# Attention with an MLP behind it: keys in three tiles of 128, and the last 64 keys of a whole batch as block-diagonal tiles

## The chip, the cores and the metric

The kernel runs on one core of a Trainium2 chip. The metric is the device time of one execution in microseconds (us); lower is better. The core has five engines with a queue each: TensorE (PE; its weight loads are listed as PEld), VectorE (DVE), ScalarE (ACT), GpSimd (POOL) and SyncE (SP), which here only issues DMAs. TensorE writes to PSUM, eight banks of 512 float32 a partition; everything else lies in SBUF.

## The reference

There are 8 batches of 12 heads with 448 tokens of 64 features. Queries and keys are normalized by their root mean square and scaled by g_q and g_k; softmax attention follows; the heads of a token are put together to 768 features; and an MLP with a gated activation ends it.

```python
def rmsnorm(x, g):
    rms = np.sqrt(np.mean(x * x, axis=-1, keepdims=True) + 1e-06)
    return x / rms * g
q_n, k_n = (rmsnorm(q, g_q), rmsnorm(k, g_k))
scores = scale * np.matmul(q_n, k_n.transpose(0, 1, 3, 2))
attn = np.exp(scores - max) ; attn = attn / sum          # over the keys
x = np.matmul(attn, v)                                   # then (8 * 448, 12 * 64)
h = x @ w_in                                             # 768 -> 2048
g = h * np.clip(h + 3.0, 0.0, 6.0) / 6.0
out = g @ w_out                                          # 2048 -> 768
```

## The kernel before

**Pairs of heads.** The unit of the attention is a pair of heads, six pairs to a batch (NJ = 6), 48 in all (P = 0 to 47). The two heads share the 128 partitions after the transposition, 64 features each.

**Stages of a pair.** `loads` (L295) brings K and Q into one tile qk and V into vf, token p*4 + t on partition p, so 112 partitions (PT) with four tokens each (T). `prep` (L310) squares K and Q (L320 to L330), sums the squares over the 64 features (L337), makes the inverse root on ScalarE (L343, L344), scales into bfloat16 qks (L351) and casts V into va (L359), which has a column of ones behind the 64 features, so that AV gives the sum of the exponentials too. `turn` (L365) turns qks so that features lie on partitions: for the first ten pairs (NPE) by TensorE (L377), for the others by a DMA transpose from SP (L388); the keys are then multiplied by g_q g_k into kp (L381 or L392). `attend` (L402) makes the scores transposed, keys on partitions: four tiles of 112 keys by 448 queries, the two heads as two matmuls in 64 rows of the array each (L416), and takes the exponential of both heads at once (L421, 112 partitions by 896). From batch 1 on two tiles are put in one step ("size = 2"), which takes both buffers of S. `gather` (L429) multiplies the exponentials by V (L437): for each of four slices of 128 queries, four key tiles for two heads, eight matmuls with 65 columns. The first three slices go to X; the last, of which only the upper 64 queries are new, goes to R, which is shared by three pairs. VectorE divides by the sums (L462, L463 for X of each pair; L502, L503 for R of three pairs), and the result is turned to xT (by TensorE in batch 0, by DMA transposes after, L486, L511). The 64 last tokens of two batches share one 128-token tile of the MLP, so even batches have 384 columns of h, odd ones 512.

**MLP.** `h_group` (L525): 16 groups a batch of six matmuls (L533), with the activation on ScalarE (L539) and VectorE (L541). `y_group` (L550): six or eight groups a batch of 16 matmuls (L558), copied by VectorE (L566) and stored by SP (L585). While batch b is in attention, TensorE's time is filled with h of batch b-1 and y of batches b-2 and b-1; what is left after the last attention runs alone at the end.

**Order.** Every piece of work is a step with a duration, a due time and the steps it depends on (class `Plan`). `order` (L68) simulates the engines with these durations and gives each engine's instructions in the order that comes out; the engines then run strictly in that order, each waiting by semaphores for what it needs. The due times come from `begin[P]`: START, then FIRST for each pair of batch 0, and after it the MLP time of the batch over six plus PAIR. `Ring` hands out buffers in turn, and the step that takes one waits for all users of what was in it. The weights of the MLP are loaded by GpSimd in eight parts (L277, L283), from W_IN_AT and W_OUT_AT on. `spare` (L599) gives the PSUM banks of the attention to the MLP at its end.

PSUM before: S two buffers of two banks, X and R one buffer of one bank each, M two of one bank.

Of the kernel before, what the change touches and what calls it, by code (L numbers as in the profile page):

```python
# [33 lines left out]
class Plan:  # L34
# [33 lines left out]
    def order(self):  # L68
# [8 lines left out]
        soft = []  # L77
# [13 lines left out]
        while len(done) < len(self.steps):  # L91
# [14 lines left out]
            for x in s.on:  # L106
                open_[x].remove(s)
            s.eng, s.start = e, at
# [3 lines left out]
            if s.xfer:  # L112
# [5 lines left out]
                else:  # L118
                    dma_free = self.hard(soft, max(dma_free, s.end), s.xfer)
                    s.end = dma_free + self.DMA_LATENCY + s.late  # L120
            done.append(s)
# [23 lines left out]
def kernel(  # L145
# [24 lines left out]
    NP = B * NJ  # L170
    assert PT == 112 and S - SM == 64 and D == 64 and NKT == NJ and B % 2 == 0
# [8 lines left out]
    mark = const.tile([1, 1], FP32, name="mark")  # L180
    ident = const.tile([128, 128], BF16, name="ident")
# [3 lines left out]
    qk_r = Ring(tiles("qk", 5, [128, 2, 2, T * D], FP32))  # L185
    vf_r = Ring(tiles("vf", 5, [128, 2, T * D], FP32))
    sq_r = Ring(tiles("sq", 2, [128, 2, 2, T * D], FP32))
    ssq_r = Ring(tiles("ssq", 4, [128, 4 * T], FP32))
    rs_r = Ring(tiles("rs", 4, [128, 4 * T], FP32))
    qks_r = Ring(tiles("qks", 3, [128, 2, T, 2, D]))  # L190
    kq_r = Ring(tiles("kq", 4, [128, 2, S]))
    kp_r = Ring(tiles("kp", 3, [128, S + 16]))
    va_r = Ring(tiles("va", 5, [128, 2, T, E1]))
    e_r = Ring(tiles("e", 3, [128, T, 2, S]))
    xn_r = Ring(tiles("xn", 3, [128, NS, 2, D]))
    rd_r = Ring(tiles("rd", 3, [128, NS, 2], FP32))
# [6 lines left out]
    X_r = Ring(tiles("X", 1, [128, 512], FP32, psum))  # L203
    R_r = Ring(tiles("R", 1, [128, 512], FP32, psum))
# [6 lines left out]
    GATE, W_IN_AT, W_OUT_AT, W_STEP = 2, 7.0, 35.0, 6.3  # L211
    START, FIRST, PAIR = 9.0, 4.1, 2.3
    LEAD = 4
    HURRY = 0.8
# [27 lines left out]
    for P in range(NP):  # L242
        b = P // NJ
        begin.append(begin[-1] + (FIRST if b == 0 else (
            sum(x[3] for x in seq[b]) / NJ + PAIR + (1.1 if (P + 2) < NPE else 0.0))))
    begin += [begin[-1] + 8.0 * (i + 1) for i in range(8)]

# [15 lines left out]
    def make_ones():  # L263
        for t in va_r.bufs:
            nc.gpsimd.memset(t[:, :, :, D:E1], 1.0)
        for t in kp_r.bufs:
            nc.gpsimd.memset(t[:, S:S + 16], 0.0)

    g_load = add("ACT", 2.2, 0, load_g, after=1.5, late=3.0)
    g_make = add("DVE", 0.1, 0, lambda: nc.vector.scalar_tensor_tensor(  # L270
        out=gp[:], in0=gq_t[:], scalar=8.0, in1=gk_t[:], op0=MULT, op1=MULT), g_load, after=7.5)
    id_make = add("POOL", 0.5, 0, make_ident)
    one_make = add("POOL", 0.6, 0, make_ones)
# [17 lines left out]
    def heads(src, P):  # L291
        b, j = divmod(P, NJ)
        return src[b, 2 * j:2 * j + 2, :, :].rearrange("h (p t) d -> p h (t d)", t=T)

    def loads(P):  # L295
        at = begin[P]
        qk, war, use = qk_r.take()
        res = []
        cost = 0.62 if P < 3 else 0.85
        for i, src in enumerate((k, q)):  # L300
            e = "ACT" if i and P < 3 else "SP"
            res.append(add(e, 0.47, at - 26, lambda i=i, src=src, e=e: {"ACT": nc.scalar, "SP": nc.sync}[e].dma_start(
                out=qk[0:PT, i], in_=heads(src, P)), *war, xfer=cost, after=max(0.7, at - 24)))
        L[P] = (qk, use, res)
        vf, war, use = vf_r.take()
        s = add("SP", 0.47, at - 19, lambda: nc.sync.dma_start(
            out=vf[0:PT], in_=heads(v, P)), *war, xfer=cost, after=max(0.7, at - 20))
        V[P] = (vf, use, s)

    def prep(P):  # L310
        at = begin[P]
        hurry = HURRY if P < NJ else 1.0
        qk, qk_use, ld = L.pop(P)
# [3 lines left out]
        def square(e, i):  # L317
            o, x = sq[0:PT, i], qk[0:PT, i]
# [5 lines left out]
        halves = P < 2 * NJ  # L324
# [72 lines left out]

    AV, XT, R = {}, {}, {}  # L400

    def attend(P):  # L402
        b, j = divmod(P, NJ)
# [270 lines left out]
```

## Time and profile before

| what | us |
|---|---|
| median of 7 runs (440.61 to 443.31) | 441.18 |
| the profiled execution | 442.12 |
| its span, first to last instruction | 440.2 |
| TensorE busy, matmuls | 412.3 (94%) |
| VectorE busy | 245.2 (56%) |
| ScalarE busy | 248.8 (57%) |
| GpSimd busy | 240.6 (55%) |
| exponentials L421, 192 of 914 ns | 166.2 |
| scaling L351 on GpSimd, 87 of 1060 ns | 90.9 |
| squares L329 on GpSimd, 36 of 1892 ns | 68.1 |
| sums L337 on VectorE, 47 of 1214 ns | 57.1 |

Busy time counts how long an engine had at least one instruction in it. For TensorE matmuls overlap in the pipeline and their ends are modelled; so what a matmul costs is read from the distance between starts. A line of the timeline gives start, duration, engine (SPq and ACTq are the queues that issue DMAs), source line, operation, output<-input with sizes, the count, and in brackets how long the engine idled before it and on what. In the chain of waits each line is a start, a duration and what was the last to end there. The granted clock of TensorE was 0.996 of full.

### The profile page before, as it was taken

To read this page: it belongs to the slowest core of one execution; us is meant where nothing else is said; L and a number is where in the kernel's file an instruction comes from. 1 tells how busy PE (TensorE), PEld (TensorE's weight loads), DVE (VectorE), ACT (ScalarE), POOL (GpSimd) and SP (SyncE) were. 2 spreads that over 40 slices of the span, in tenths; PEclk is the share of its full clock that TensorE was granted. 3 is DMA by queue.
4 is the path that set the end of the run, shared out by engine and by line. 5 is a ranking of instruction groups with operands and counts; after the bars stand their busy time and mean duration, and the time that the engine had idled before them with its cause. 6 is when DMAs were issued, how large, how long until landed. Compare 5 with 4: busy or idle time off the path is not lost.

```text
span 440.2 us, 9224 instructions
## 1 busy us (share of the span) xinstructions
PE 412.3 (94%) x3682; PEld 229.1 (52%) x3682; DVE 245.2 (56%) x417; ACT 248.8 (57%) x425; POOL 240.6 (55%) x230
## 2 busy tenths in 40 slices
PE   0687889999999999999999999999999999999996
PEld 0355445555455565554455555554455555654563
DVE  1998777657664564456565465456564444334421
ACT  3788578557775676357673677457673665123200
POOL 3499899765857657665766666746757510000000
PEclk9999899999999999999999999999999999999999
DMA  8999999988464746674456655684466320220122
GB/s 233 251 264 259 228 222 195 191 191 206 104 141 131 187 118 141 150 213 126 116 163 166 163 140 156 159 209 117 107 162 175 95 57 11 56 80 0 37 71 73
DMA packets 102923, 64.58 MB, mean 147 GB/s; under 512 B 59744, under 2 KB 99424, under 8 KB 102880
## 3 DMA queue, kind: packets, MB, share of 16 engines
q1 hardware_dynamic: 94544, 57.01, 51.6%
q0 software_dynamic: 7296, 6.29, 8.9%
q10 hardware_dynamic: 1040, 0.69, 0.5%
q8 instruction: 29, 0.48, 0.5%
q14 instruction: 14, 0.11, 0.1%
HBM read 45.61 MB, written 11.01 MB: 129 GB/s over the span
## 4 chain that ended last, share of the span: by engine, by line
PE 76%; DVE 7%; POOL 5%; issue 5%; ACT 3%; DMA 3%; SPq 1%; POOLq 0%; DVEq 0%
PE M L558 25%; PE M L533 24%; PE S L416 8%; PE X L437 7%; PE S L558 4%; PE S L533 2%; DVE ssq L337 2%; POOL sq L329 2%; PE R L437 2%; ACT e L421 2%; DMA qk<-in_k_dram 1%; DVE qks L351 1%; POOL qks L351 1%; PE X L558 1%; DVE sq L322 1%
## 5 line engine op out<-in xcount | busy, mean ns | idle before, releaser
L421 ACT ACTIVATE e<-S 112x896 bf16<-112x896 f32 x192 | 166.2, 914 | 64.9 <-PE S L416 64.9
L533 PE MATMUL M<-xT,w_in_sb 128*128 128x384 bf16 (+1 forms) x696 | 147.9, 351 | 3.8 <-DVE gT L541 3.8
L351 POOL TENSOR_TENSOR qks<-qk,rs 112x512 bf16<-112x512 f32 x87 | 90.9, 1060 | 89.0 <-ACT rs L344 88.9
L558 PE MATMUL M<-w_out_sb,gT 128*128 128x384 bf16 x736 | 131.8, 326 | 0.0
L558 PEld LDWEIGHTS <-gT 128*128 128x128 bf16 x896 | 82.9, 98 | 57.8 <-issue 7.8
L533 PEld LDWEIGHTS <-w_in_sb 128*128 128x128 bf16 x768 | 69.8, 98 | 69.2 <-issue 14.5
L541 DVE SCALAR_TENSOR_TENSOR gT<-t,M 128x384 bf16<-128x384 f32 (+1 forms) x116 | 70.7, 611 | 59.9 <-ACT t L539 59.1
L539 ACT ACTIVATE t<-M 128x384 f32<-128x384 f32 (+1 forms) x116 | 62.6, 540 | 68.7 <-PE M L533 65.2
L437 PEld LDWEIGHTS <-e 112*128 112x128 bf16 x1536 | 64.9, 99 | 31.4 <-issue 16.0
L337 DVE TENSOR_REDUCE ssq<-sq 112x16 f32<-112x1024 f32 (+1 forms) x49 | 58.3, 1192 | 24.4 <-POOL sq L329 12.0
L329 POOL TENSOR_TENSOR sq<-qk 112x1024 f32<-112x1024 f32 x36 | 68.1, 1892 | 0.0
L416 PE MATMUL S<-kq,kp 64*128 64x448 bf16 x384 | 56.6, 364 | 3.9 <-DVE kp L381 1.7
L437 PE MATMUL X<-va,e 112*128 112x65 bf16 x1152 | 58.4, 195 | 0.8 <-ACT e L421 0.6
L566 DVE COPY y<-M 128x384 f32<-128x384 f32 x46 | 25.6, 556 | 59.3 <-PE M L558 59.1
L359 POOL CAST va<-vf 112x512 bf16<-112x512 f32 x48 | 31.6, 659 | 9.0 <-DMA vf<-in_v_dram 7.2
L392 POOL TENSOR_SCALAR kp<-kq,gp 128x448 bf16<-128x448 bf16 x23 | 32.3, 1402 | 5.6 <-DMA kq<-qks 5.6
L463 DVE TENSOR_TENSOR xn<-X,rd 128x384 bf16<-128x384 f32 x48 | 26.7, 557 | 1.6
L416 PEld LDWEIGHTS <-kp 64*128 64x128 bf16 x384 | 12.3, 94 | 28.0 <-issue 19.0
L437 PE MATMUL R<-va,e 112*128 112x65 bf16 x384 | 20.4, 195 | 0.0
L377 PE MATMUL M<-ident,qks 112*128 112x112 bf16 x80 | 7.8, 238 | 13.0 <-DVE qks L351 12.4
L558 PE MATMUL S<-w_out_sb,gT 128*128 128x384 bf16 x112 | 19.5, 326 | 0.0
L462 DVE RECIPROCAL rd<-X 128x6 f32<-128x6 f32 x48 | 9.2, 191 | 15.8 <-PE X L437 15.8
(42 smaller groups left out, 155.0 us busy)
## 6 DMA issues: line engine op xcount, KB each, us to landing
qk<-in_k_dram SPq DMA_DIRECT2D x48, 224.0 KB, 3.4
vf<-in_v_dram SPq DMA_DIRECT2D x48, 224.0 KB, 3.6
qk<-in_q_dram SPq DMA_DIRECT2D x45, 224.0 KB, 3.6
w_in_sb<-in_moe_w_in_dram POOLq DMA_DIRECT2D x4, 768.0 KB, 11.7
w_out_sb<-in_moe_w_out_dram POOLq DMA_DIRECT2D x4, 768.0 KB, 10.8
out_dram<-y SPq DMA_DIRECT2D x8, 336.0 KB, 3.1
out_dram<-y SPq DMA_DIRECT2D x8, 288.0 KB, 3.2
out_dram<-y SPq DMA_DIRECT2D x8, 240.0 KB, 3.6
```

The source lines that it names most:

```text
L329: parts = [add("POOL", 1.93, at - 10, lambda: nc.gpsimd.tensor_tensor(out=sq[0:PT], in0=qk[0:PT], in1=qk[0:PT], op=MULT), *ld, *war, lock= ...
L337: red = add("DVE", 0.6 * n, at - 8 * hurry + 0.5 * i0, lambda i0=i0, i1=i1, cs=cs: nc.vector.tensor_reduce(out=ssq[0:PT, cs], in_=sq[0:PT, ...
L351: sc.append(add(on, 0, at - 6 * hurry, lambda e, i=i, rs4=rs4: engines[e].tensor_tensor(out=qks[0:PT, i].rearrange("p t h d -> p h t d"), ...
L359: vc = add({"POOL": 0.61}, 0, at - 3, lambda e: engines[e].tensor_copy(out=va[0:PT, :, :, 0:D], in_=vf[0:PT].rearrange("p h (t d) -> p h t ...
L392: nc.vector if e == "DVE" else nc.gpsimd).tensor_scalar_mul(
L416: nc.tensor.matmul(out=ps[:, a, 0:S], lhsT=kp[rows, c0:c0 + 128], rhs=kq[rows, 1, :], start=True, stop=True)
L421: x = add("ACT", 0.93, at + step * (t0 + i) / T + 0.2, lambda t=t0 + i, ps=ps: nc.scalar.activation(out=e[0:PT, t], in_=ps[0:PT, :, 0:S], ...
L437: nc.tensor.matmul(out=dst[:, a * E1:(a + 1) * E1], lhsT=e[0:PT, t, a, c0:c0 + 128], rhs=va[0:PT, a, t, :], start=(first and a == 0 and t ...
L533: nc.tensor.matmul(out=m[:, 0:n], lhsT=w_in_sb[:, kt, f * 128:(f + 1) * 128], rhs=X[:, kt, :], start=(kt == 0), stop=(kt == NKT - 1))
L539: r = add("ACT", 0.08 + n / 1200, due + span, lambda: nc.scalar.activation(out=t[:, 0:n], in_=m[:, 0:n], func=RELU, bias=0.5, scale=1.0 / ...
L541: g = add("DVE", 0.12 + n / 960, due + span, lambda: nc.vector.scalar_tensor_tensor(out=G[:, f, :], in0=t[:, 0:n], scalar=1.0, in1=m[:, 0: ...
L558: nc.tensor.matmul(out=m[:, 0:HALF], lhsT=G[:, f, i * 128:(i + 1) * 128], rhs=w_out_sb[:, f, cols], start=(f == 0), stop=(f == NFT - 1))
```

## The change

K and V are no longer dealt out as four tiles of 112 keys. The first 384 keys of a head form three tiles of 128 (token p*3 + t on partition p); the last 64 keys of all twelve heads of a batch are loaded, normalized and turned together, once a batch. For these, each pair gets a tile `kb` of 128 features by 128 keys that is zero outside two blocks, head 0 in the upper left and head 1 in the lower right, so that one matmul with all 128 rows gives the scores of both heads' rest keys, head 0 on partitions 0 to 63, head 1 on 64 to 127. Their AV runs as 64-row matmuls, one head in each half of the array, in the same step as a cluster of scores, and opens the accumulation in X. X now has two banks (one for each head) with all four slices, and R is gone. Q stays in four tiles of 112 queries.

From batch 1 on, two pairs are planned together: a cluster of two score tiles, one of the rest keys of both pairs (both in one S tile, one exponential), and two more of two tiles. The normalization of the last slice comes with each pair. In the planner, DMAs of SP and ACT wait for the eighth before them; the loads of the g vectors come first on ACT; Q of pair 0 is loaded from SP; odd pairs are prepared earlier by 0.7 of a pair's time; START stays at 9.0, FIRST goes from 4.1 to 3.7, PAIR from 2.3 to 2.1, W_IN_AT from 7 to 6, W_OUT_AT from 35 to 33.

```diff
+            if s.xfer and e != "POOL":
+                at = max(at, lanes[-8])
...
+                    lanes.append(s.end)
...
-    X_r = Ring(tiles("X", 1, [128, 512], FP32, psum))
-    R_r = Ring(tiles("R", 1, [128, 512], FP32, psum))
+    X_r = Ring(tiles("X", 1, [128, 2, 512], FP32, psum))
...
-    g_load = add("ACT", 2.2, 0, load_g, after=1.5, late=3.0)
+    g_load = add("ACT", 1.95, -99, load_g, after=0.7, late=1.0)
...
-            e = "ACT" if i and P < 3 else "SP"
+        e = "ACT" if 0 < P < 3 else "SP"
...
+    def rest_loads(b):
...
+            x = src[b, :, SM:S, :].rearrange("(j h) p d -> h p j d", h=2)
+            return [add("SP", 0.5, at, lambda a=a: nc.sync.dma_start(out=dst[a * 64:a * 64 + 64], in_=x[a]), *war,
+                        xfer=0.7, after=max(0.7, begin[b * NJ] - 30)) for a in range(2)]
...
+    def rest_prep(b):
...
+            q1 = add("POOL", 0.8, at - 12, lambda: nc.gpsimd.tensor_tensor(
+                out=sqr[:], in0=kr[:], in1=kr[:], op=MULT), *kl, *war, lock=True)
+        red = add("DVE", 0.47, at - 8 * hurry + 3, lambda: nc.vector.tensor_reduce(
+            out=rsr[:, 0:NJ], in_=sqr[:], axis=AX_X, op=ADD), q1, *rwar)
...
+        mk = add("DVE", 0.1, at - 6 * hurry + 3, lambda: nc.vector.tensor_tensor(
+            out=rm, in0=rsr[:, NJ:2 * NJ].unsqueeze(2).to_broadcast([128, NJ, 2]),
+            in1=head[:].unsqueeze(1).to_broadcast([128, NJ, 2]), op=MULT), r, head_make, lock=True)
+        on = {"DVE": 0.9} if b == 0 else {"DVE": 0.9, "POOL": 1.6}
+        sc = add(on, 0, at - 6 * hurry + 3, lambda e: (nc.vector if e == "DVE" else nc.gpsimd).tensor_tensor(
+            out=krs[:], in0=kr[:].unsqueeze(2).to_broadcast([128, NJ, 2, D]),
+            in1=rm.unsqueeze(3).to_broadcast([128, NJ, 2, D]), op=MULT), mk, *kwar, lock=True)
...
+            tr = add("SP", 1.3, at - 6, lambda: nc.sync.dma_start_transpose(
+                out=kb[:], in_=krs[:].rearrange("p j h d -> p (j h d)")), sc, *bwar, xfer=1.4, late=1.5)
+            ks = add("DVE", 0.47, at - 2, lambda: nc.vector.tensor_scalar_mul(
+                kb[:].rearrange("p j c -> p (j c)"), kb[:].rearrange("p j c -> p (j c)"), gp[:, 0:1]), tr, g_make,
+                lock=True)
...
+    def rest_keys(P):
...
+            for s in range(NS + 1):
+                c0 = s * 128 if s < NS else S - 128
+                for a in range(2):
+                    rows = slice(a * 64, a * 64 + 64)
+                    nc.tensor.matmul(
+                        out=X[:, a, s * E1:(s + 1) * E1], lhsT=er[rows, i, c0:c0 + 128], rhs=var[rows, P % NJ, :],
+                        start=(s == 0), stop=False, skip_group_check=True)
...
+    def attend_two(P, part):
+        step = (begin[P + 2] - begin[P]) / 7
+        if part == 0:
+            open_pair(P)
+            attend([[[(P, 0)], [(P, 1)]]], (0, P - 1), begin[P], step)
+        else:
+            open_pair(P + 1, (AV[P][2], AVR[P], AV[P][3]))
+            for cluster, extra, x in (
+                    ([[(P, NS), (P + 1, NS)]], None, POS[0]),
+                    ([[(P, 2)], [(P + 1, 0)]], (0, P), POS[1]),
+                    ([[(P + 1, 1)], [(P + 1, 2)]], None, POS[2])):
+                attend([cluster], extra, begin[P] + x * 7 * step, step)
...
-        size = 1 if P < NJ else 2
-        for t0 in range(0, T, size):
...
             for a in range(2):
-                for t in range(T):
+                for t in range(NS):
                     nc.tensor.matmul(
-                        out=dst[:, a * E1:(a + 1) * E1], lhsT=e[0:PT, t, a, c0:c0 + 128], rhs=va[0:PT, a, t, :],
-                        start=(first and a == 0 and t == 0), stop=(t == T - 1), skip_group_check=True)
+                        out=X[:, a, s * E1:(s + 1) * E1], lhsT=e[:, t, a, c0:c0 + 128], rhs=va[:, a * NS + t, :],
+                        start=False, stop=(t == NS - 1), skip_group_check=True)
...
+        av = [add("PE", 0.2, at + 0.25 * step * s, lambda s=s: values(s), rest, *exps.values(), vc)
+              for s in range(NS + 1)]
```

In `attend` (new signature: clusters of tiles, an optional pair whose rest AV goes in, a due time) each cluster is one TensorE step that waits for all S tiles, keys, the X banks and the rest exponential of its members; `attend_first` does the pairs of batch 0 one tile at a time, each with a rest exponential of its own of 448 columns, and `attend_last` the rest AV of pair 47. POS is (0.22, 0.44, 0.75) and AV_AT (0.04, 0.26, 0.46, 0.4), as shares of the time of two pairs.

## The prediction

> **What bounds the kernel now.** I read three views in this order: busy shares by window, to cut the run into stages; the timeline, for what one step costs there; the waits, for what ends last.
>
> Busy microseconds of each engine in six stretches (columns: stretch, PE, weight loads, VectorE, ScalarE, GpSimd, granted clock, DMA share, GB/s):
>
> ```profile
> core 0: us, PE busy (x) PEld busy (x) DVE busy (x) ACT busy (x) POOL busy (x), PEclk, DMA share, GB/s
> 9.50:44.80 35.30, 25.18 (x320) 15.29 (x322) 33.25 (x57) 28.16 (x50) 28.08 (x29) 0.99 1.15 256
> 44.80:132.00 87.20, 84.21 (x808) 45.57 (x808) 60.57 (x100) 60.56 (x106) 64.89 (x60) 0.98 0.90 184
> 181.70:231.40 49.70, 49.70 (x434) 25.77 (x433) 28.19 (x47) 31.78 (x54) 34.10 (x30) 1.00 0.58 151
> 231.40:281.10 49.70, 49.70 (x466) 29.12 (x464) 27.47 (x48) 29.51 (x52) 31.89 (x29) 1.00 0.59 157
> 380.50:440.00 59.50, 55.36 (x322) 30.23 (x320) 20.22 (x34) 9.55 (x16) 0.00 (x0) 1.00 0.19 53
> ```
>
> To 44.8 us (batch 0, no MLP beside it) VectorE is the full engine, 94%, GpSimd next. From 132 to 380.5 us TensorE is busy without a gap, and no other engine exceeds 69% of its stretch. The tail from 380.5 us is MLP alone. Busy matmuls overlap, so I check TensorE by starts. The chain of waits repeats its pattern at the same place two batches apart:
>
> ```profile
> 143.03 1.95 PE M L533 x12
> ...
> 243.41 1.95 PE M L533 x12
> ...
> 342.80 1.95 PE M L533 x12
> ```
>
> That is 100.4 and 99.4 us for two batches, 49.7 for one. One batch has 96 h matmuls (0.163 us at 384 columns, 0.216 at 512, from the spacing of starts) and 96 or 128 y matmuls of 0.163: on average 18.2 and 18.2, 36.4 us of MLP. The other 13.3 us are six head pairs, 2.22 us each. The timeline of one such place prices them:
>
> ```profile
> 202.71 1.03 PE L533 MATMUL M<-xT,w_in_sb 128*128 128x512 bf16 x4
> 203.67 0.55 PE L416 MATMUL S<-kq,kp 64*128 64x448 bf16 x4
> 204.16 0.69 PE L437 MATMUL X<-va,e 112*128 112x65 bf16 x16
> 204.68 2.10 PE L533 MATMUL M<-xT,w_in_sb 128*128 128x512 bf16 x9
> 206.62 0.42 PE L437 MATMUL X<-va,e 112*128 112x65 bf16 x8
> 206.89 0.81 PE L533 MATMUL M<-xT,w_in_sb 128*128 128x512 bf16 x3
> ```
>
> The four h matmuls end at 202.71 + 4 x 0.216 = 203.575; AV starts at 204.16. So a cluster of two score tiles costs 0.585: 0.374 for twice 448 columns with the two heads side by side, and 0.21 fixed. Eight AV matmuls cost 206.89 - 206.62 = 0.27, and 16 cost 0.52: 0.265 a slice, 0.033 a matmul. Twice 0.585 plus four times 0.265 is 2.23, the 2.22 above.
>
> For the start, the timeline and the waits:
>
> ```profile
> 4.32 0.53 ACTq L254 DMA_DIRECT2D gq_t<-in_g_q_dram  x1
> 4.89 0.60 ACTq L255 DMA_DIRECT2D gk_t<-in_g_k_dram  x1
> 7.06 0.47 ACTq L254 DMA_DIRECT2D gq_t<-in_g_q_dram  x1
> 8.37 0.47 ACTq L255 DMA_DIRECT2D gk_t<-in_g_k_dram  x1
> 8.88 1.67 ACT L320 ACTIVATE sq<-qk 112x512 f32<-112x512 f32 x3 [6.88 <-DMA gq_t<-in_g_q_dram]
> 14.13 0.93 PE L416 MATMUL S<-kq,kp 64*128 64x448 bf16 x4 [1.23 <-DVE kq L383]
> ```
>
> The first key load is issued at 0.73 and lands 3.6 us later, at 4.3. ScalarE squares it only at 8.88: its queue stands at the four loads of the g vectors, the last issued at 8.37. Eight DMAs of SP and ACT are under way by 3.2 us and the ninth is issued at 4.32: eight outstanding look like the limit.
>
> **What the Trainium skill says.** *TensorEngine Tiling (Array Packing)*, Key Properties: changing the tiling mode drains the array, while tiles work independently. The trace agrees: 0.21 us fixed for a 64-row cluster, none for a 112-row AV between h matmuls, and four 64-row matmuls in the time of two. *TensorE: Matmul & The Clock Gate*, "Wait — 56ns, not 53.3ns?": starts never come closer than about 25 ns; here 65 columns cost 33. *DMA: Bandwidth & Descriptors*, Specifications: below 512 B a transfer loses line rate; the new rest loads have 256 B rows, and no run of before shows such loads.
>
> **The change part by part.**
>
> *Scores.* Columns are the same: four tiles of 112 keys become three of 128 and half of a block-diagonal tile (one 128-row matmul gives both heads' 64 rest keys). What falls is the clusters. Two pairs now take three 64-row clusters and one full-row cluster of two rest matmuls: 3 x 0.585 + 2 x 0.187 = 2.13, 1.06 a pair against 1.17: -0.11. I count no drain for the full-row one, as AV shows none.
>
> *AV.* Before, 32 matmuls; now 24 of 128 rows (0.795 us) and eight of 64 rows for the rest keys, put behind the scores in an open 64-row cluster. The latter isn't in the trace: at best the two heads run side by side, 4 x 0.033 = 0.13; at worst one after the other, 0.265. I take 0.16, nearer to the best because scores do run side by side, and keep both ends. AV: 0.955 against 1.06, -0.105.
>
> *Sum for TensorE.* -0.21 us a pair for the 42 pairs of batches 1 to 7: -8.8 (ends: -0.11 x 42 = -4.5, and -0.24 x 42 = -10.1). The last pair has a rest cluster of its own, 0.21 + 0.13 = +0.3. So -8.5.
>
> *ScalarE.* Four exponentials of 914 ns a pair become three and a half; -0.46 us a pair at 59 to 64% use: nothing behind TensorE, slack in batch 0, where each rest exponential covers 448 columns alone (half of 914, so 0.5).
>
> *VectorE and GpSimd.* Per pair the prepared elements fall from 1024 to 896 per partition: squares 1.89 to 1.65 on GpSimd (now two instructions), scaling 2.12 to 1.86, V cast 0.66 to 0.5, the sum 1.21 to 1.06 on VectorE, kp 448 to 384 columns. Normalizing R once per three pairs (0.2 + 0.56) becomes 0.25 every pair. Per batch come a square 0.8, a reduce 0.45, a mask 0.15, a doubled scaling 0.9 (VectorE) or 1.6, kb 0.5 to 0.85, a cast 0.5: about 4 us, some 0.65 a pair, estimated from the rows of 512 elements by size. It balances what is saved. In the TensorE-bound stage it is hidden at 55 to 69% use; without that cover it would cost up to 0.65 a pair.
>
> *Loads.* K and V rows of 768 B instead of 1024, 6/7 of the bytes; per batch four loads of 64 x 6 rows of 256 B, and one more transpose. Even if a 256 B row costs as much as 1 KB, the rows grow from 4032 a batch to 5952, DMA share from 0.58 to at most 0.58 x 5952/4032 = 0.86. Free after 132 us; before that DMA is the busiest resource, and the end +2 of the next step holds it. In SP's queue five more issues a batch of 0.5 to 1.2 us stand ahead of some xT and kq transposes; SP issues for 13.7 of the 25 us from 193, so 3 us a batch fit in.
>
> *Start.* g moves to the front of ACT's queue, and pair 0's q load to SP. By about 2.7 us both are issued with the rest keys: eight DMAs, four of them tiny. The first square can then begin when k lands, near 4.4 instead of 8.88: -4.5. From there batch 0 is work of VectorE and GpSimd, 61 us in the 35.3 us stretch. In it I save about 6.5 us (an eighth of squares, scalings and sums of nine pairs) and add about 6 (rest preparation of batches 0 and 1, mostly VectorE): even. Of the 4.5 I take 4.0; ends -7 (the ScalarE slack counts too) and +2 (the rest work lands on full VectorE and the start is limited by loads).
>
> *44.8 to 132.* TensorE needs 80.7 (MLP 52, pairs 26.7, transposes 2) of 87.2. I keep that loss as it is and charge +1 for new waits anywhere, as a score cluster now waits also for the rest exponential and for the X banks.
>
> *Sum.* The profiled execution took 442.1 (span 440.2 and 1.9 around it): 442.1 - 8.5 - 4.0 + 1.0 = 430.6. The median is 0.9 below that execution: 429.7.
>
> **The rivals.**
>
> *B, the start gives nothing.* For it: VectorE at 94% gets the rest preparation. Against: ScalarE's 4.5 us are plain waiting. 442.1 - 8.5 - 0.9 + 1 = 433.7.
>
> *C, the row tiles of AV don't run side by side* or cost a drain of their own. For it: at 33 ns a matmul the AV is near a floor of issue, not of columns. Against: the pairs of scores. Only -0.11 x 42 stays: 442.1 - 4.5 + 0.3 - 4 + 1 - 0.9 = 434.
>
> *D, slower: the X accumulator.* X and R were apart; now X takes both banks, one buffer, and the next pair's rest AV, inside a score cluster, waits until VectorE has normalized the pair before. Behind that cluster stands all of TensorE's queue. From the last AV of a pair to the next cluster there is about a quarter of 15 us for two pairs, 3.8 us; VectorE needs 0.4 wait, 0.2 + 0.56 + 0.25 work and whatever (up to 1.2, the sum) runs ahead. It decides if a pair loses over 12/42 = 0.3 us. If half the pairs miss by 1 us, +21: 451. Against: VectorE is 55% used and the wait before, `rd` for AV, was the other way round.
>
> That the change doesn't do what it says I see no room for: the tiles are sized in it.
>
> **How the numbers follow.** Both gains, 424 to 435: 0.62. B 0.14, C 0.09, D 0.13, and 0.02 for losses that just cancel. The forecast is 429.7. The range 423 to 438 takes in A, B, C with the ends of TensorE's sum, and leaves out D and the tails. About 0.3% (1.3 us) can be told from no change. Faster 0.84, same 0.03, slower 0.13.
>
> **What would show it.** Right: the spacing of the pattern near 48.4 instead of 49.7; clusters of score, rest AV and next matmul 0.12 to 0.16 apart for the rest AV; first square near 4.4 and first score near 9 to 10; end of batch 0 near 41. Wrong: gaps on TensorE before a score cluster with VectorE's normalization or ScalarE's exponential as releaser (D), rest AV at 0.27 (C), the first h matmul still at 45.7 (B), or waits for the loads of the rest keys.

## The result, and the profile after

The changed kernel takes 445.05 us (median of 14 runs, 443.1 to 449.76), the kernel before in the same sessions 441.47: a ratio of 1.0091, 95% interval 1.0069 to 1.0112. It is slower by about 4 us where 11.5 us less was forecast. Ratios and intervals in this document are of fast executions alone: one that is over 1.5% above the fastest of its kernel is left out of them. The profiled execution of the changed kernel took 447.43 us, 2.4 above its median, with a span of 445.7; that of before has 440.2.

The same five stretches as before, now of the changed kernel (columns: stretch, PE, weight loads, VectorE, ScalarE, GpSimd, granted clock, DMA share, GB/s):

```profile
9.50:44.80 35.30, 25.49 (x262) 15.50 (x261) 25.72 (x49) 22.87 (x45) 25.78 (x31) 0.76 1.17 243
44.80:132.00 87.20, 74.19 (x734) 41.44 (x731) 62.35 (x109) 51.78 (x95) 63.61 (x76) 0.98 1.01 190
181.70:231.40 49.70, 49.41 (x457) 27.42 (x456) 30.15 (x55) 29.57 (x55) 32.58 (x39) 1.00 0.66 154
231.40:281.10 49.70, 49.01 (x456) 28.94 (x454) 30.12 (x55) 28.23 (x53) 30.41 (x37) 1.00 0.68 162
380.50:440.00 59.50, 59.50 (x359) 33.09 (x355) 20.55 (x35) 9.91 (x17) 0.00 (x0) 1.00 0.19 52
```

Before, VectorE was busy for 33.25 us of the first stretch and TensorE for 84.21 us of the second. Now it is 25.72 and 74.19, the granted clock of the first is 0.76 where it was 0.99, and the DMA share of the second went from 0.90 to 1.01. So these engines do less in the same time and wait more, and they wait before 132 us. (The DMA share sums the times of all packets over 16 engines, so it can exceed 1.) A row for some of the head pairs says when the ground is lost. These are the starts of VectorE's normalization of a pair in both traces, in us:

| pair | before | after | difference |
|---|---|---|---|
| 0 | 23.1 | 20.8 | -2.3 |
| 3 | 35.6 | 40.8 | +5.2 |
| 6 (batch 1 begins) | 49.9 | 61.6 | +11.7 |
| 12 | 94.3 | 102.8 | +8.5 |
| 18 | 140.0 | 153.3 | +13.3 |
| 30 | 240.4 | 251.0 | +10.6 |
| 42 | 339.8 | 348.7 | +8.9 |
| 46 | 372.6 | 378.7 | +6.1 |

From pair 18 on the change does most of what was forecast (96.8): two batches take 97.7 us (pairs 18 to 30, and 30 to 42) where they took 100.4 and 99.4. Before that it loses 13.3 us. The loss begins inside batch 0, with 5.2 us at pair 3, and is 11.7 us at pair 6. The lines for pair 6, first before, then after:

```profile
49.86 0.56 DVE L463 TENSOR_TENSOR xn<-X,rd 128x384 bf16<-128x384 f32 x1
...
61.58 0.56 DVE L675 TENSOR_TENSOR xn<-X,rd 128x384 bf16<-128x384 f32 x1
```

What the forecast said of the very first step came true. The timeline of ScalarE in the changed kernel, and TensorE's first scores:

```profile
4.63 0.52 ACT L355 ACTIVATE sq<-kf 128x384 f32<-128x384 f32 x1 [2.63 <-DMA gq_t<-in_g_q_dram]
...
8.72 0.52 ACT L355 ACTIVATE sq<-kf 128x384 f32<-128x384 f32 x1 [1.75 <-DMA kf<-in_k_dram]
```

```profile
11.31 0.93 PE L568 MATMUL S<-kq,kp 64*128 64x448 bf16 x4 [2.59 <-DVE kq L432]
```

The first square starts at 4.63 in place of 8.88, but the first scores only at 11.31 in place of 14.13, where 9 to 10 was forecast: VectorE copies kq at 10.88, behind the sum of pair 1 (9.79), and before that sum it stood for 1.85 us until pair 1's squares were made. By pair 3 the lead has turned into a loss. Windows of ten microseconds each, first of the kernel before, then of the changed kernel:

```profile
25.00:35.00 10.00, 8.45 (x142) 5.72 (x139) 9.35 (x18) 8.69 (x16) 9.48 (x11) 1.00 1.15 266
35.00:45.00 10.00, 7.44 (x104) 4.56 (x105) 8.78 (x18) 7.90 (x11) 10.00 (x11) 0.95 1.17 261
```

```profile
25.00:35.00 10.00, 6.20 (x56) 3.42 (x56) 6.38 (x15) 5.40 (x11) 3.55 (x6) 0.61 1.17 251
35.00:45.00 10.00, 7.60 (x91) 5.17 (x91) 6.88 (x14) 5.68 (x11) 9.53 (x12) 0.53 1.15 258
```

GpSimd, busy for 9.48 of the 10 us from 25 us on, is now at 3.55. The DMA share lies between 1.15 and 1.17 in all four rows: in the row from 25 us no engine of the changed kernel is full, but the DMA engines are as busy as before. What GpSimd stands at is in its timeline, and the chain of waits of the changed kernel runs through the same loads:

```profile
24.29 0.82 POOL L479 TENSOR_TENSOR sqr<-kr 128x384 f32<-128x384 f32 x1 [0.29 <-DMA kr<-in_k_dram]
27.00 1.14 POOL L357 TENSOR_TENSOR sq<-qf 112x512 f32<-112x512 f32 x1 [1.90 <-DMA qf<-in_q_dram]
30.77 0.50 POOL L409 CAST va<-vf 128x384 bf16<-128x384 f32 x1 [2.63 <-DMA vf<-in_v_dram]
...
39.47 1.47 POOL L494 TENSOR_TENSOR krs<-kr,rsr 128x768 bf16<-128x768 f32 x1
```

```profile
23.08 11.63 DMA qf<-in_q_dram
...
52.94 0.33 DVE kb L513
...
56.29 14.20 DMA qf<-in_q_dram
```

Two q loads alone stand for 25.8 us of that chain. The rest keys of batch 1 go through the same place: their K loads land at 24.1 us, GpSimd scales them at 39.47, the transposing DMA lands at 49.1, VectorE makes kb at 52.9, and TensorE's first rest scores of batch 1 wait for that:

```profile
53.33 0.55 PE L573 MATMUL S<-kq,kb 128*128 128x448 bf16 x2 [0.47 <-DVE kb L513]
```

### The profile page after: what moved, and what is told of

The parts are those of the page before. It is cut to its first block, busy times and chain, and to the rows that moved or that the text cites. A ratio compares the mean times of both kernels' runs of the same rounds, so it can differ in the third digit from the quotient of the medians.

```text
span 445.7 us, 9320 instructions
## 1 busy us (share of the span) xinstructions
PE 407.9 (92%) x3630; PEld 232.7 (52%) x3630; DVE 255.7 (57%) x464; ACT 233.8 (52%) x421; POOL 233.4 (52%) x289
## 3 DMA queue, kind: packets, MB, share of 16 engines
q1 hardware_dynamic: 116256, 58.62, 58.2%
## 4 chain that ended last, share of the span: by engine, by line
PE 71%; DMA 11%; DVE 10%; POOL 3%; SPq 2%; issue 2%; ACT 1%; POOLq 0%; DVEq 0%
PE M L761 24%; PE M L736 23%; DMA qf<-in_q_dram 8%; PE X L656 7%; PE S L568 5%; PE S L761 4%; PE S L736 2%; DVE ssq L373 2%; PE X L761 2%; DVE gT L744 2%; PE S L573 2%; POOL sq L357 2%; PE X L736 1%; DVE xn L675 1%; DMA vr<-in_v_dram 1%
## 5 line engine op out<-in xcount | busy, mean ns | idle before, releaser
L601 ACT ACTIVATE e<-S 128x896 bf16<-128x896 f32 x144 | 124.8, 916 | 37.6 <-PE S L568 37.3
L409 POOL CAST va<-vf 128x384 bf16<-128x384 f32 x48 | 24.9, 522 | 82.9 <-PE X L656 51.5
L656 PEld LDWEIGHTS <-e 128*128 128x128 bf16 x1152 | 54.8, 101 | 23.0 <-issue 4.9
L373 DVE TENSOR_REDUCE ssq<-sq 128x14 f32<-128x896 f32 (+2 forms) x49 | 52.0, 1061 | 18.8 <-POOL sq L357 11.3
L656 PE MATMUL X<-va,e 128*128 128x65 bf16 x1152 | 61.4, 198 | 0.2 <-ACT e L601 0.2
L357 POOL TENSOR_TENSOR sq<-qf 112x512 f32<-112x512 f32 x41 | 43.8, 1069 | 7.0 <-DMA qf<-in_q_dram 7.0
L394 POOL TENSOR_TENSOR qks<-qf,rs 112x512 bf16<-112x512 f32 x42 | 43.9, 1045 | 2.6 <-ACT rs L380 2.6
L387 POOL TENSOR_TENSOR qks<-kf,rs 128x384 bf16<-128x384 f32 x45 | 37.9, 843 | 9.5 <-ACT rs L380 7.5
L357 POOL TENSOR_TENSOR sq<-kf 128x384 f32<-128x384 f32 x42 | 35.1, 837 | 5.5 <-DMA kf<-in_k_dram 4.0
L442 POOL TENSOR_SCALAR kp<-kq,gp 128x384 bf16<-128x384 bf16 x24 | 30.3, 1262 | 13.8 <-PE S L568 9.5
L379 ACT ACTIVATE rs<-ssq 128x14 f32<-128x14 f32 (+2 forms) x49 | 10.6, 217 | 33.4 <-DVE ssq L373 33.2
## 6 DMA issues: line engine op xcount, KB each, us to landing
w_in_sb<-in_moe_w_in_dram POOLq DMA_DIRECT2D x4, 768.0 KB, 11.7
```

The lines of the kernel that those rows point to most:

```text
L357: engines[e].tensor_tensor(out=o, in0=x, in1=x, op=MULT)
L373: lambda i0=i0, i1=i1, rows=rows: nc.vector.tensor_reduce(out=ssq[0:rows, i0:i1], in_=sq[0:rows, i0:i1], axis=AX_X, op=ADD),
L387: engines[e].tensor_tensor(out=qks[:, 0:NS].rearrange("p t (h d) -> p h t d", h=2), in0=kf[:].rearrange("p (h t) d -> p h t d", h=2), in1= ...
L394: engines[e].tensor_tensor(out=qks[0:PT, NS:QB].rearrange("p t (h d) -> p h t d", h=2), in0=qf[0:PT].rearrange("p (h t) d -> p h t d", h=2 ...
L601: lambda dst=dst, ps=ps, w=2 if whole else 1: nc.scalar.activation(out=dst, in_=ps[:, 0:w, 0:S], func=EXP), s, *(AVW[P] if t < NS else AVR ...
L656: nc.tensor.matmul(out=X[:, a, s * E1:(s + 1) * E1], lhsT=e[:, t, a, c0:c0 + 128], rhs=va[:, a * NS + t, :], start=False, stop=(t == NS - ...
```

## The experiments

The expectations speak of theories (letters of their own, not the prediction's rivals). A: the DMA engines hold the start, through the rows of the new loads. B: the added work on VectorE and GpSimd holds it. C: the new rule of eight outstanding loads makes a worse order. D: the faster pace in the planner (3.7 and 2.1) puts work for far pairs ahead of near ones. P, added later: the orders were made for landings that the planner takes too early. Times are medians; "before" is the kernel before in the same session. It lies between 441.5 and 442.7 in all of them, so medians of different sessions are set side by side.

**e1, rest keys loaded once.** Batches 1 to 7 use the rest keys and values that batch 0 loaded.

```diff
+        if b:
+            REST[b] = ONCE[0]
+            return
         at = begin[b * NJ]
         kr, war, k_use = kr_r.take()
```

> The rest loads of K and V are made for batch 0 only and its tile is used for all batches (so batches 1 to 7 are computed with the wrong rest keys); preparation of the rest tiles stays. Theory A (the start is held by transfers: loads of the rest keys stand ahead of pair loads while the DMA engines are full and eight transfers are out): 28 loads of about 1 us less, 8 of them before 60 us; 445 falls to 433 to 438. Theory B (VectorE and GpSimd are held by the added preparation): no change, 443 to 446. Theory C (the planner's new rule for DMAs gives a worse order): no change either.

Measured: 445.29 (ratio 1.0076, 1.0049 to 1.0103). A missed its figure: pair 6 came at 66.8. GpSimd stood for 6.2 us at one of the pair loads, until 34.5 us. Taking the loads away changed the order too, so the run alone doesn't decide.

**e2, rest loads later** (due 18 and 10 us ahead of their batch in place of 30 and 29).

```diff
-        k_at, v_at = (-24.5, -18.5) if b == 0 else (-30, -29)
+        k_at, v_at = (-24.5, -18.5) if b == 0 else (-18, -10)
```

> Same transfers, but from batch 1 on the rest loads are due 18 and 10 us before their batch instead of 30. Theory A in the form that their place in SP's queue matters: 437 to 441. In the form that their volume matters: 443 to 446. Theory B: 443 to 446.

Measured: 445.27 (1.0071, 1.0036 to 1.0107). Their place in the queue isn't it.

**e3, weights later.**

```diff
-    GATE, W_IN_AT, W_OUT_AT, W_STEP = 2, 6.0, 33.0, 6.3
+    GATE, W_IN_AT, W_OUT_AT, W_STEP = 2, 16.0, 45.0, 6.3
```

> Weights of the MLP 10 and 12 us later (W_IN_AT 6 to 16, W_OUT_AT 33 to 45), same bytes. Theory A: pair loads land sooner in the first 40 us, 437 to 442, unless the weights are then late themselves. Theory B: no change, 443 to 446.

Measured: 446.19 (1.0103, 1.007 to 1.0136). No gain.

**e4, without the rule of eight loads.**

```diff
-                at = max(at, lanes[-8])
+                pass
```

> The planner's rule that a DMA waits for the eighth before it is taken out; all else as changed. Theory C: 438 to 442. Theories A and B: not faster, 444 to 450, since the rule only describes what the chip does.

Measured: 454.12 (1.0288, 1.0261 to 1.0314). The rule brings about 9 us; C falls. The trace of the changed kernel shows what the rule stands for: never are more than eight DMAs of SP and ACT under way.

**e5, the constants of before** (and 1.1 for 1.0 in the pairs turned on TensorE).

```diff
-    GATE, W_IN_AT, W_OUT_AT, W_STEP = 2, 6.0, 33.0, 6.3
-    START, FIRST, PAIR = 9.0, 3.7, 2.1
+    GATE, W_IN_AT, W_OUT_AT, W_STEP = 2, 7.0, 35.0, 6.3
+    START, FIRST, PAIR = 9.0, 4.1, 2.3
```

> The change with the planner's constants of before (FIRST 4.1, PAIR 2.3 and 1.1, W_IN_AT 7, W_OUT_AT 35). Theory D (the faster planned pace orders work for far pairs ahead of work for near ones, and the engines stand at loads that have not landed): 438 to 442. Theory A (the DMA engines are full at the start, whatever the plan): 443 to 447.

Measured: 449.67 (1.0166, 1.0109 to 1.0222). D falls in this form.

**e6, the doubled scaling of the rest keys on GpSimd from batch 1 on.**

```diff
-        on = {"DVE": 0.9} if b == 0 else {"DVE": 0.9, "POOL": 1.6}
+        on = {"DVE": 0.9} if b == 0 else {"POOL": 1.6}
```

> From batch 1 on the doubled scaling into krs runs on GpSimd only. If the 1.75 us of it on VectorE are what holds the MLP's activation back once a batch after 150 us, two batches take 96.5 to 97.2 instead of 97.7 and the run 441 to 444; if the wait only moves to another instruction, 444 to 446.

Measured: 443.42 (1.0025, 1.0005 to 1.0045), 1.6 us below the changed kernel, as expected. Two batches of the TensorE-bound stage take 96.8 us (pairs 18 to 30 and 30 to 42) where the changed kernel takes 97.7. The tile view of krs from 130 us on, first of the changed kernel, then of e6 (duration ns min/median/max):

```profile
L494 DVE TENSOR_TENSOR krs<-kr,rsr x4: 958/1489/1752, 156.1 to 302.4; 128x768 bf16<-128x768 f32 x4
```

```profile
L494 POOL TENSOR_TENSOR krs<-kr,rsr x4: 1472/1472/1472, 153.8 to 298.4; 128x768 bf16<-128x768 f32 x4
```

The planner priced it at 0.9 on VectorE; it takes up to 1.75 there, and the activation gT stands behind it. In the chain of waits of the changed kernel it stands ahead of the h matmuls at two places a hundred us apart:

```profile
156.12 1.75 DVE krs L494
...
158.39 1.14 PE M L736 x6
...
253.86 1.75 DVE krs L494
...
256.13 1.14 PE M L736 x6
```

That krs is the cause of the whole 0.9 us isn't shown: e9 below, with krs on VectorE at 1.2 to 1.6 us in this stage, takes 97.1 and 97.0 for two batches, and e10, with krs on GpSimd, 98.5 and 97.0.

**e7 and e8, V loaded for the first five pairs only**, in the changed kernel and in the kernel before.

```diff
-        V[P] = (vf, use, load_tiled(at - 19, vf, v, P, war, cost, max(0.7, at - 20)))
+        if P < 5:
+            VL.append(load_tiled(at - 19, vf, v, P, war, cost, max(0.7, at - 20)))
+        V[P] = (vf, use, VL[P % 5])
```

> V is loaded for the first five pairs only and their tiles are used again (the output has the wrong values of V), so a third of the pair loads is gone. Theory A: the start is no longer held by transfers and the gain that the prediction had counted shows against the same edit of the kernel before: 9 to 14 us less than that one. Theory B (work of VectorE and GpSimd): still 2 to 6 us more than that one. Theory D: between, about equal.

> The same edit of the kernel before (V loaded for the first five pairs only, so the output has wrong values of V). Its start had slack in its loads: 437 to 441 under each theory; the difference to the changed kernel with this edit is what counts.

Measured: e7 446.11 (1.0089, 1.0051 to 1.0126), e8 441.82 (0.9982, 0.9959 to 1.0005). e7 lies 4.3 us above e8, within the 2 to 6 that B had named and far from A's figure. V loads hold neither kernel; in e7 the rest loads of batch 1 still stand ahead of K and Q from 11 to 19 us.

**The plan against the trace.** The program plans every load's issue and landing before it emits an instruction. Load by load of the changed kernel's SP queue, in us:

```
load              planned issue, landing    measured issue, landing    late
15 vf             9.1   17.2                10.9   19.0                 1.8
17 kr (batch 1)  10.4   18.9                12.0   24.1                 5.2
21 vr (batch 1)  13.4   22.9                17.0   29.7                 6.8
28 vf            21.3   29.5                29.0   40.8                11.2
31 qf            25.5   33.1                32.9   44.3                11.2
```

In the kernel before the lag is at most 5.9 us and gone at 39 us. The reason is in `hard`: a pair load is charged at the slow rate only for weight loads that were issued when it was priced. The next runs repair that.

**e9, true landings.** As long as weight loads are to come, the rest of a transfer is charged at the slow rate, and a rest load at 0.96. **e10** adds e6's edit. **e12** is the kernel before with the same repair.

```diff
-        return at + todo
+        return at + (todo / self.HARD if more and soft else todo)
...
-                    dma_free = self.hard(soft, max(dma_free, s.end), s.xfer)
+                    dma_free = self.hard(soft, max(dma_free, s.end), s.xfer, len(soft) < 8)
```

> Edit in the planner alone: while weight loads are still to be issued, a pair load is charged at the slower rate for the whole of its transfer (before, only weight loads already issued when it was priced counted), and a rest load costs 0.96 instead of 0.7. The planned landings up to 60 us then lie near the real ones of the changed kernel (load 28: 44.3 planned, 40.8 real, where the plan said 29.5). Theory P (the orders of GpSimd, VectorE and SP were made for landings that came 5 to 12 us too early, and only the order costs time): 431 to 438 us, and no stretch of 25 to 36 us in which all engines stand. Theory A (the DMA engines cannot bring the rows sooner, whatever order stands behind them; the plan with true landings itself ends 13 us later than the plan of the changed kernel): 442 to 446, pair 18 normalized at 148 to 154.

> The planner edit of the true landings, and the doubled scaling of the rest keys on GpSimd from batch 1 on. If the two losses add (start by landings, stage by the VectorE operation of 1.75 us), it is 1.5 to 2 us below the kernel with the first edit alone, as the second edit alone was below the changed kernel. Theory P: 429 to 436; theory A: 440 to 444.

> The kernel before with the planner edit of the true landings. Its loads came at most 5.9 us later than planned and were on plan again at 39 us. Theory P (mis-timed landings cost time where they are many): within 2 us of the kernel before, 440 to 443. If the planner edit itself brings or costs something whatever the loads, it shows here.

Measured: e9 445.75 (1.008, 1.0053 to 1.0108), e10 445.33 (1.0075, 1.0041 to 1.011), e12 443.85 (1.0033, 1.0012 to 1.0055). In e9 loads 16 to 42 now land within 1.8 us of the plan, and the time is the same: P falls. With the landings known the loads simply are that late. Two things changed within that time, though. In batch 0 the loss is gone: pair 3 is normalized at 34.1 in e9 and 33.1 in e10, where before had 35.6 and the changed kernel 40.8. All of it comes at pair 6 instead, at 66.8 and 64.0. And e10 missed its own figure: it was to lie 1.5 to 2 us below e9 and lies 0.4 below, less than the intervals can tell. The windows of e9:

```profile
25.00:35.00 10.00, 7.34 (x102) 4.39 (x101) 8.92 (x21) 7.06 (x13) 4.34 (x7) 0.87 1.19 236
35.00:45.00 10.00, 5.34 (x56) 3.29 (x57) 7.51 (x16) 3.78 (x9) 2.69 (x5) 0.50 1.21 236
```

**e11, neither V nor rest loads** (the edits of e1 and e7 together, old planner).

> V is loaded for the first five pairs only and the rest keys for batch 0 only, and used again after that; all computing steps stay. It leaves about half of the rows of the loads away. Theory A (rows of the loads bound the start): 430 to 437, all engines busy at 25 to 36 us. Theory B (VectorE and GpSimd bound the start and what follows): above 442, with VectorE or GpSimd over 90% busy to 130 us. Theory P: between, since the plan has fewer loads to misjudge.

Measured: 443.45 (0.9978, 0.9941 to 1.0015; single runs from 438 to 448, the traced one 444.85). It is muddled: as the rest keys are at hand from the start, the planner scales the rest keys of five batches before 130 us. From the groups of VectorE between 10 and 130 us of e11 (busy us, mean ns, idle before; the mean hides that three of the five took 0.95 us, one 2.58 and one 6.45):

```profile
L500 DVE TENSOR_TENSOR krs<-kr,rsr 128x768 bf16<-128x768 f32 x5 | 11.9, 2374 | 0.0
```

B as a second limit behind the loads is possible but not shown by this run. It asks for runs in which each is removed under the true landings.

**e13, e14, e15: the loads alone.** e13 is e10 with e1's edit. e14 is e10 with the weights at 16 and 40 us and the old pace:

```diff
-    GATE, W_IN_AT, W_OUT_AT, W_STEP = 2, 6.0, 33.0, 6.3
-    START, FIRST, PAIR = 9.0, 3.7, 2.1
+    GATE, W_IN_AT, W_OUT_AT, W_STEP = 2, 16.0, 40.0, 6.3
+    START, FIRST, PAIR = 9.0, 4.1, 2.3
```

e15 is e12 with the four rest loads a batch added into tiles that nobody reads:

```diff
+            return [add("SP", 0.5, at, lambda a=a: nc.sync.dma_start(out=dst[a * 64:a * 64 + 64], in_=x[a]), *war,
+                        xfer=0.96, after=max(0.7, begin[b * NJ] - 30)) for a in range(2)]
...
+        k_use += load(k, kr, at + k_at, war)
+        v_use += load(v, vr, at + v_at, vwar)
```

> Planner with true landings, doubled scaling on GpSimd from batch 1 on, and the rest keys loaded for batch 0 only (later batches use batch 0's rest keys; all computing steps stay). It stands beside e10, 445.3, which differs in the rest loads alone. Theory A (the rows of the rest loads hold the start): 434 to 439, with pair 6 normalized before 56. Theory B (the work on the rest keys holds it): 443 to 446, VectorE over 95% busy from 25 to 65 us.

> As e10, but the weight loads start at 16 and 40 us in place of 6 and 33, and the planner spaces the pairs by the constants of the kernel before (4.1 and 2.3). Nothing is left out. Theory A: loads of the first 20 pairs that stood at 10 to 15 us of flight land earlier, pairs 3 to 6 come earlier, 438 to 441. Theory B: no change against e10, 444 to 446.

> The kernel before with true landings in its planner, and with four rest loads a batch (64 partitions of six rows of 256 bytes each) put beside its own loads, into tiles that nobody reads. Nothing else is added. It stands beside e12, 443.9. Theory A: 450 to 463, the loss before 130 us. Theory B (the loads are hidden, the work on the rest keys costs the time): 443 to 446.

Measured: e13 440.01 (0.9936, 0.9909 to 0.9963), 5.3 us below e10. e14 444.94 (1.0079, 1.0056 to 1.0101): no change against e10 that can be told. e15 465.99 (1.0559, 1.0506 to 1.0611), 22 us above e12; pair 6 comes at 60.2 instead of 50.5, pair 18 at 163.6 instead of 142.7, and after that nothing more is lost. So with loads that nobody waits for the kernel before comes 9.7 us later to pair 6, where the whole change costs 11.7. The 22 us are not a clean price of the rows, though: the planner, which charges them, also ordered 96 y matmuls in one piece from 81.0 to 96.8 us and left the next pairs without MLP beside them. The nearest to a price under equal work is e13's 5.3 us. It isn't clean either: e13's plan has scaled the rest keys of batches 1 to 5 by 128 us, e10's those of batches 1 to 3 by 110. And e13 still has pair 6 at 66.3, so the loads aren't the whole. In its trace the transposing DMA of batch 1 is issued at 41.7 us and lands 10.0 later, but VectorE, busy for 7.93 of the 9.10 us from then on, scales kb only at 60.8:

```profile
L515 SPq DMA_TRANSPOSE kb<-krs x1: 1333/1333/1333, 41.7 to 41.7; - x1
L517 DVE TENSOR_SCALAR kb<-kb,gp x1: 407/407/407, 60.8 to 60.8; 128x768 bf16<-128x768 bf16 x1
```

**e16, no rest work.** Loads and work of the rest keys only for batch 0, whose kb and var all batches use; TensorE does all that it does in the changed kernel. True landings. **e18** leaves both out for batches 1 and 2 only; it also has e6's edit, like e10.

```diff
     def rest_loads(b):
+        if b:
+            return
...
     def rest_prep(b):
+        if b:
+            REST[b] = REST[0]
+            return
```

> The rest keys are loaded and prepared for batch 0 only, and every later batch uses batch 0's normed rest keys and values: their loads and their work on VectorE, GpSimd and ScalarE are left out from batch 1 on, while TensorE does all that it does in the changed kernel. The planner knows the true landings. Theory A alone (only the loads cost): as e13, 438 to 441. Theories A and B together (loads about 5 us, work on full VectorE and GpSimd the rest of the 11 us): 430 to 435, near the forecast of 429.7, with pair 6 normalized before 58.

> As e10 (true landings, doubled scaling on GpSimd; 445.3), with the loads of and the work on the rest keys left out for batches 1 and 2 only, which use batch 0's; batches 3 to 7 have their own. If the 12.5 us between e10 and e16 are lost where DMA engines and VectorE are full (up to 130 us): 432 to 435. If each batch pays its part wherever it stands: two sevenths of 12.5, so 441 to 442.

Measured: e16 432.8 (0.9781, 0.974 to 0.9821; four runs within 0.6 us), e18 438.62 (0.992, 0.9893 to 0.9947). Starts of the normalization, in us:

| pair | before | e10 | e13, no loads | e18, none for b 1, 2 | e16, none |
|---|---|---|---|---|---|
| 6 | 49.9 | 64.0 | 66.3 | 50.3 | 49.4 |
| 10 | 80.7 | 90.3 | 89.0 | 83.4 | 83.6 |
| 16 | 124.7 | 132.2 | 127.7 | 125.7 | 122.2 |
| 46 | 372.6 | 376.2 | 369.7 | 368.6 | 364.0 |

Without rest work pair 6 is back at 49.4:

```profile
49.39 0.56 DVE L680 TENSOR_TENSOR xn<-X,rd 128x384 bf16<-128x384 f32 x1
```

The windows of e16:

```profile
25.00:35.00 10.00, 6.61 (x91) 4.14 (x88) 9.84 (x21) 6.28 (x13) 4.19 (x6) 0.83 1.18 246
35.00:45.00 10.00, 7.50 (x135) 5.08 (x132) 8.08 (x19) 7.34 (x12) 7.89 (x10) 1.00 1.18 252
45.00:55.00 10.00, 8.73 (x78) 5.11 (x71) 8.46 (x15) 6.97 (x16) 8.87 (x11) 1.00 1.22 238
```

The clock of 35 to 45 us is 1.00 (0.50 in e9), GpSimd at 7.89 (2.69 in e9), though the DMA engines are as full. From e10 to e16 it is 12.5 us. That is what loads and work of the rest keys of batches 1 to 7 cost together, with what the planner makes of the room. If e13's 5.3 us are taken for the loads, 7.2 are left for the work on them. e18 lies between what it expected of both cases: 6.7 of the 12.5 us belong to batches 1 and 2. Between pairs 10 and 16 it loses another 3.5 us against e16, where batch 3's rest keys are prepared and the DMA share is still 1.07 (105 to 115 us). In the profiled executions only 1.1 us more separates it from e16 by pair 46, for batches 4 to 7.

What within the work takes the 7.2 us, the busy time or the length of its chain, no run separates. The tile view of kb in e10 shows how long the chain is: the transposing DMA is issued at 38.4, lands 16.1 us later, and VectorE scales kb at 58.2. In e13 the greater part of the wait, 9 us, comes after the landing.

```profile
L511 SPq DMA_TRANSPOSE kb<-krs x1: 6457/6457/6457, 38.4 to 38.4; - x1
L513 DVE TENSOR_SCALAR kb<-kb,gp x1: 548/548/548, 58.2 to 58.2; 128x768 bf16<-128x768 bf16 x1
...
DMA to landing us min/median/max: 16.1/16.1/16.1
```

In the changed kernel batch 0's rest keys are turned on TensorE instead, between 12.2 and 13.0 us. Turning batch 1's there as well wasn't tried.

**e17, squares of pairs 3 to 7 on ScalarE**, beside e6's edit.

```diff
-                {"DVE": 0.68 * c, "POOL": 1.04 * c} if P < 2 * NJ else {"POOL": 1.04 * c})
+                {"ACT": 0.63 * c} if P < 8 else {"DVE": 0.68 * c, "POOL": 1.04 * c} if P < 2 * NJ else {"POOL": 1.04 * c})
```

> As e6 (443.4), with the squares of pairs 3 to 7 on ScalarE (6 to 7 of 10 us busy there) in place of VectorE and GpSimd. Nothing is left out. Theory B as a part of the loss: 439 to 442. Theory A alone: 443 to 444, since the loads come no sooner.

Measured: 445.2 (1.0062, 1.0038 to 1.0086), 1.8 us above e6. ScalarE's idle time brought nothing there. No version that computes everything came out below the kernel before; e6 is the nearest.

## Why the prediction was wrong

- **TensorE's sum, -0.21 us a pair: right.** Two batches, twelve pairs, went from 99.9 us (mean of 100.4 and 99.4) to 96.8 in e6 and e16: -0.26 a pair. In the changed kernel it is 97.7, -0.18 a pair; krs on VectorE may be a reason, but that isn't shown. From pair 6 to pair 46 e16 gains 8.1 us; the sum had 8.5.
- **Rest AV at 0.16, between 0.13 and 0.265: too dear.** In the timeline of the changed kernel six h matmuls of 0.163 from 269.04 end at 270.02, and the next ones start at 270.71. That is 0.69; less the 0.585 of a score cluster it is 0.11 for eight matmuls:

```profile
269.04 1.14 PE L736 MATMUL M<-xT,w_in_sb 128*128 128x384 bf16 x6
270.11 0.55 PE L568 MATMUL S<-kq,kp 64*128 64x448 bf16 x4
270.50 0.28 PE L540 MATMUL X<-var,er 64*128 64x65 bf16 x8
270.71 0.66 PE L736 MATMUL M<-xT,w_in_sb 128*128 128x384 bf16 x3
...
273.25 0.54 PE L573 MATMUL S<-kq,kb 128*128 128x448 bf16 x2
273.63 0.35 PE L656 MATMUL X<-va,e 128*128 128x65 bf16 x6
```

  The full-row rest scores take 273.63 - 273.25 = 0.38, twice 0.187 and no drain, as forecast. Rival C (row tiles not side by side) didn't occur.
- **Rival D, the X accumulator, didn't occur.** In the stage from 181.7 to 281.1 us TensorE idles for 1 us in all.
- **The start, -4.0 with ends of -7 and +2: this step failed.** It was worth +11.7 us at pair 6 and +13.3 at pair 18, far outside its ends. The first square at 4.4 was right (4.63); of the 4.5 us that it was to gain 2.8 were left at the first scores. What was wrong is the sentence after: "I save about 6.5 us ... and add about 6 ...: even". It set busy time against busy time. What is saved lies in every pair, but what is added for batch 1 lies in a chain (load, square, sum, inverse root, scaling, transposing DMA, kb, rest scores) that must end before the second cluster of pairs 6 and 7, and this chain runs where the DMA engines are full and VectorE nearly so. In the changed kernel the first cluster of pair 6 starts at 46.12, and the rest scores follow only at 53.33. e16, without the chain from batch 1 on, has them at 42.83 and pair 6 at 49.4, where before had 49.9. A low clock isn't needed for the loss at pair 6: in e10 it is 1.00 from 25 to 35 us and 0.73 from 35 to 45, above the 0.61 and 0.53 of the changed kernel, and pair 6 comes at 64.0 all the same.
- **The loads, "free after 132 us", with "the end +2" before: the term was mis-sized.** The rows were counted rightly (4032 to 5952 a batch) and DMA was named as the busiest resource, but 1,920 more rows a batch on full DMA engines were charged, with the rest work, 2 us at most. Rest loads and rest work together measure 12.5 us (e10 against e16); the 1,536 rows a batch that are rest loads come to about 5.3 of them (e10 against e13).
- **The forecast itself.** With the rest keys' loads and work left out from batch 1 on, e16 takes 432.8: that is what TensorE's part is worth, near rival B (433.7, the start gives nothing). Even then pair 6 comes only 0.5 us earlier than before. The slower side had a chance of 0.13, all of it on the accumulator. The rest keys stood in the prediction as busy time (about 4 us a batch) and as a last sign of being wrong, waits for their loads; they were not made a rival with a price.

## What to carry to other kernels

Work that is taken out of every step and gathered into one batch-wide chain must be priced by when that chain can end: with its transfers at the times that they take from issue to landing in that stretch (10.3 to 13.5 us for batch 1's rest loads in the changed kernel, up to 16.1 for the transposing DMA in e10, where the first K load of the kernel before took 3.6), and with its steps at their places in the order of a busy engine. Busy time alone is not the price. Where the DMA engines are full, count rows against the stretch in which they fall: in e15 loads that nobody reads delayed pairs that nobody had changed. When removing a suspect brings nothing, look first whether the program re-plans around it; e1 and e13 remove the same loads, and only the second, under true landings, shows their 5.3 us.

## What the runs showed of the hardware

- **With weight loads in flight, SP's loads got rows, not bytes.** In the kernel before the ten loads that landed from 19 to 30 us brought 2,240 rows in 11.2 us, in the changed kernel the seven loads that landed from 19 to 29.7 us brought 2,272 rows in 12.7 us (each counted from the landing ahead of them): 200 and 179 rows a microsecond, but 205 and 80 GB/s, as four of the seven are rest loads with rows of 256 bytes. The Trainium skill, *DMA: Bandwidth & Descriptors*, Queues, rings and completion order, says that a DMA engine serves the queues that have work in turn, a packet at a time. The row rates fit this; how many rows make a packet here no run shows.
- **Never more than eight DMAs of SP and ACT were under way.** That holds in the traces of both kernels and of e4. In the changed kernel SP issues load 28 at 29.02 us, when load 20 has landed at 29.01, load 31 at 32.87 (load 23 landed at 32.80) and load 35 at 38.76 (load 27 landed at 38.70). So a slow landing also holds back the issue eight places behind it.
- **TensorE's clock halved without an idle window, and for long.** In the changed kernel TensorE stands from 25.0 to 27.6 us for kq, and the clock goes to 0.50 and stays there up to 44 us. Windows of three microseconds, columns as above:

```profile
23.00:26.00 3.00, 1.99 (x39) 1.56 (x35) 0.82 (x3) 1.81 (x5) 1.81 (x3) 1.00 1.18 257
26.00:29.00 3.00, 1.40 (x10) 0.68 (x11) 2.93 (x8) 0.81 (x1) 1.14 (x1) 0.71 1.17 243
29.00:32.00 3.00, 2.75 (x35) 1.88 (x34) 2.00 (x5) 2.49 (x8) 1.24 (x2) 0.50 1.18 233
...
41.00:44.00 3.00, 3.00 (x35) 1.90 (x32) 1.47 (x5) 2.54 (x3) 3.00 (x4) 0.50 1.12 272
```

  The Trainium skill, *TensorE: Matmul & The Clock Gate*, What's actually happening, gives half rate after an idle window of about 3.4 us. Here the longest gap is 2.61 us; in e9, where the clock falls to 0.50 at 32.5 us, no gap in the 3.4 us ahead of it is longer than 0.76, and TensorE is busy for 2.06 of the 3.40 us from 29.00. So on this record no idle window was needed. How much work keeps the clock up, and what share of the loss the low clock has, was not separated.
- **Two-input operations of VectorE stretch beside GpSimd.** The scaling of q on VectorE took 0.68 us at best and 2.61 at worst in the first 140 us of the changed kernel (GpSimd was busy for 2.13 of those 2.61). krs took 0.96 at 104.49, with GpSimd idle, and 1.75 at 156.12, with GpSimd busy for 0.94 of it. The Trainium skill, *Trainium Architecture — The Big Picture*, What this means for kernel authors, says that the two share a port pair by an exclusive lock; these durations agree with it. A price taken from an undisturbed operation, as the planner's 0.9 for krs, is too low where both engines are busy.
